# Ties between GpSimd and VectorE for a shared port: from the first quarter of an instruction list to all of it

## The chip, the core and the metric

The kernel runs on one core of a Trainium2 chip. The engines of the core are called here as the profile calls them: PE (TensorE, matmuls), DVE (VectorE), ACT (ScalarE), POOL (GpSimd) and SP (SyncE, which issues nearly all DMAs). Each engine works through its own instructions in order; between engines they wait on semaphores. The metric is the device time of one execution in microseconds (us); smaller is better. Three runs of the kernel before took 605.10, 605.38 and 605.64 us; the median is 605.38 us.

## The reference

What is computed is sparse attention (a band of local positions and a few global ones) over 4 batches, 8 heads, 768 positions of 64 numbers, followed by a layer norm and a two-layer feed-forward net that is added to its input. All in float32:

```python
scores = scale * np.matmul(q, k.transpose(0, 1, 3, 2))
scores = scores + bias[None, :, :, :]          # -slope of the head * distance
scores = np.where(keep, scores, -1000000000.0) # keep = is_global | is_local
a = np.exp(scores - np.max(scores, axis=-1, keepdims=True))
a = a / (np.sum(a, axis=-1, keepdims=True) + 1e-09)
x = np.matmul(a, v)                            # heads side by side: 4 x 768 x 512
xn = (x - mu) / np.sqrt(var + 1e-06) * g_ln
out = x + np.maximum(xn @ w_ch1, 0.0) @ w_ch2  # 512 -> 2048 -> 512
```

## The kernel before

The 4 x 768 positions are cut into 24 tiles of 128. For each tile `attention` (lines 604 to 690) loads q, k and v, splits each number into two float16 parts, gets scores on PE (line 641), takes the masked minimum on DVE (line 500) and the exponentials on ACT (line 505), splits these too (lines 646 and 647), has a DMA transpose them (line 649) and multiplies them with v (lines 468 to 470). Lines 664 to 698 are the layer norm and the transposes for the feed-forward net. The net is done for pairs of tiles. For the first pairs it is plain (`ffn1_alone`, `ffn1` and `ffn2`, lines 754 to 802 and 1042 to 1066); from the fifth pair on, `seven`, `twice` and `both_` (lines 805 to 1039) do two tiles with seven products in place of eight. These need sums and differences of weight blocks: `combine` (lines 704 to 748; line 716 adds, line 730 takes the low part) and `combine2` (lines 896 to 940; line 911 adds, line 932 takes the low part) build them, beside attention and plain net, on DVE and POOL. Tiles in SBUF live in one big tile, `arena`; PSUM tiles are `bank`.

**What sets the order.** Every step is recorded first (`Plan.op`) with the engine it is for, the time it is thought to take and, in `port`, whether it uses the port that DVE and POOL share. A table written out in the kernel (`STEPS`) gives the order of all 2,319 steps; a second one (`HOMES`) says which of DVE, ACT and POOL does a step that more than one could do. `Plan.times` (lines 158 to 175) works out a planned start for each, in which steps with `port` come one after another, never two at once. The instructions are then emitted in the order of the planned starts, so each engine's own order is fixed. A step of DVE that reads PSUM has `port` false, and so have small steps, such as line 476 or the `pow` of line 492 on POOL.

On the chip the engines do not keep to the planned times; only the order within an engine and the semaphores hold. `tied` (lines 1178 to 1189) adds one kind of semaphore wait that no data asks for. `ahead` holds the DVE step with `port` that was emitted last; the next POOL step with `port` waits until that one is done:

```python
if not o.port or at_ >= TIED:
    return o.emit()
...
if o.engine == "DVE":
    ahead[:] = [new[-1].name]
elif ahead:
    tc.add_manual_dep(new[0], ahead.pop(), SYNC, reason="port")
```

`at_` is the planned start in us. With `TIED = 150.0` this holds for about the first quarter of the list. A wait goes one way: POOL for DVE. A DVE step with `port` never waits for a POOL step in this manner.

Of the kernel before, what the change touches and what calls it, by code (L numbers as in the profile page):

```python
# [180 lines left out]
def banded(ctx, tc, q, k, v, n_global, n_local, g_ln, w1, w2, out, flag):  # L181
# [996 lines left out]
    def tied(at_, o):  # L1178

        if not o.port or at_ >= TIED:  # L1180
            return o.emit()
# [30 lines left out]
        emit(line[last:])  # L1212
    return found

TIED = 150.0
IDLE, HOLD, FILL = 3, 130.0, 0.9
CW = 4
ORDER = ["t01", "t23", "w0", "w1", "w2", "w3", "w4", "w5", "w6", "w7", "w8", "w9", "w10", "w11", "w12", "w13", "w14", "w15", *(f"a{t}{j}" for t in range(4) for j in range(4))]
# [318 lines left out]
```

## Time and profile before

| | |
|---|---|
| median of three runs | 605.38 us |
| the profiled execution, its own time | 604.78 us |
| its span (first to last instruction) | 603.0 us |
| PE busy | 588.1 us, 98% of the span |
| DVE busy | 517.4 us, 86% |
| ACT busy | 334.2 us, 55% |
| POOL busy | 230.3 us, 38%, 228 instructions |
| granted clock of PE | 0.997 of full speed over the span |

The profile is of one execution. Times in it are us from the start of the span. A row of the timeline gives start and duration, engine, line, operation, what is written and read with shapes, and in square brackets how long the engine was idle before and what ended that. A row of the waits says which instruction sat idle for which other one: total, times, longest. A row of the stretches gives the length and then the busy time of PE, of PE's weight loads, of DVE, ACT and POOL, each with its number of instructions, the granted clock of PE, the share of the DMA engines and GB/s.

### The profile page before, as it was taken

To read this page: it belongs to the slowest core of one execution; us is meant where nothing else is said; L and a number is where in the kernel's file an instruction comes from. 1 tells how busy PE (TensorE), PEld (TensorE's weight loads), DVE (VectorE), ACT (ScalarE), POOL (GpSimd) and SP (SyncE) were. 2 spreads that over 40 slices of the span, in tenths; PEclk is the share of its full clock that TensorE was granted. 3 is DMA by queue.
4 is the path that set the end of the run, shared out by engine and by line. 5 is a ranking of instruction groups with operands and counts; after the bars stand their busy time and mean duration, and the time that the engine had idled before them with its cause. 6 is when DMAs were issued, how large, how long until landed. Compare 5 with 4: busy or idle time off the path is not lost.

```text
span 603.0 us, 18624 instructions
## 1 busy us (share of the span) xinstructions
PE 588.1 (98%) x7657; PEld 513.3 (85%) x7657; DVE 517.4 (86%) x1147; ACT 334.2 (55%) x819; POOL 230.3 (38%) x228
## 2 busy tenths in 40 slices
PE   9899999999999999899999999999999999999995
PEld 7889987556778756788999999999999999998995
DVE  4999899989979999999997998988998897879661
ACT  4998887765635453663662872762664663551210
POOL 1315434145454353651541641352753441353100
PEclk9999999999999999999999999999999999999998
DMA  8995999987952967779889979987999796642201
GB/s 251 260 303 140 243 233 243 194 185 132 164 111 59 161 119 151 133 148 168 159 167 178 157 155 148 150 151 152 174 149 162 135 169 127 108 83 37 68 2 58
DMA packets 260268, 91.74 MB, mean 152 GB/s; under 512 B 250192, under 2 KB 250448, under 8 KB 260176
## 3 DMA queue, kind: packets, MB, share of 16 engines
q1 hardware_dynamic: 259888, 90.47, 77.2%
q8 instruction: 62, 1.02, 0.7%
q14 instruction: 30, 0.25, 0.2%
q10 hardware_dynamic: 288, 0.00, 0.0%
HBM read 38.01 MB, written 6.29 MB: 73 GB/s over the span
## 4 chain that ended last, share of the span: by engine, by line
PE 76%; DVE 14%; ACT 3%; issue 3%; DMA 2%; POOL 1%; SPq 0%; DVEq 0%; POOLq 0%; ACTq 0%
PE bank L973 13%; PE bank L954 11%; PE bank L1053 9%; PE bank L817 7%; PE bank L819 7%; PE bank L818 7%; PE bank L641 5%; PE bank L1174 2%; PE bank L794 2%; PE bank L792 2%; PE bank L793 2%; PE bank L766 2%; PE bank L764 1%; PE bank L765 1%; PE bank L468 1%
## 5 line engine op out<-in xcount | busy, mean ns | idle before, releaser
L203 ACT ACTIVATE arena<-arena 128x512 f16<-128x512 f32 (+3 forms) x115 | 69.3, 619 | 54.7 <-DVE arena L716 12.9
L203 ACT ACTIVATE arena<-bank 128x512 f16<-128x512 f32 (+1 forms) x95 | 55.3, 591 | 70.3 <-PE bank L819 41.8
L973 PE MATMUL bank<-w2h,arena 128*128 128x256 f16 x512 | 93.3, 273 | 0.0
L817 PE MATMUL bank<-arena 128*128 128x128 f16 x512 | 87.9, 219 | 1.2 <-ACT bank L203 1.1
L819 PE MATMUL bank<-arena 128*128 128x128 f16 x512 | 87.9, 219 | 0.0
L818 PE MATMUL bank<-arena 128*128 128x128 f16 x512 | 87.9, 219 | 0.0
L1053 PE MATMUL bank<-w2h,arena 128*128 128x512 f16 x256 | 81.7, 379 | 0.9 <-DVE x L1063 0.9
L505 ACT ACTIVATE arena<-arena,mn 128x256 f32<-128x256 f32 x160 | 80.0, 501 | 3.7
L973 PEld LDWEIGHTS <-arena 128*128 128x128 f16 x768 | 72.9, 98 | 7.8
L954 PEld LDWEIGHTS <-arena 128*128 128x128 f16 x672 | 63.8, 98 | 8.1 <-issue 0.7
L973 PE MATMUL bank<-w2l,arena 128*128 128x256 f16 x256 | 69.8, 273 | 0.0
L1053 PEld LDWEIGHTS <-arena 128*128 128x128 f16 x384 | 36.1, 98 | 38.6 <-issue 1.2
L817 PE MATMUL bank<-arena,w 128*128 128x128 f16 x384 | 66.7, 219 | 0.7 <-DVE arena L867 0.6
L819 PE MATMUL bank<-arena,w 128*128 128x128 f16 x384 | 66.8, 219 | 0.0
L818 PE MATMUL bank<-arena,w 128*128 128x128 f16 x384 | 66.7, 219 | 0.0
L647 POOL TENSOR_TENSOR arena<-arena 128x512 f16<-128x512 f32 x39 | 48.1, 1236 | 43.0 <-ACT arena L203 23.4
L500 DVE CUSTOM_DVE_ANT_0 arena<-bank,mask 128x256 f32<-128x256 f32 x160 | 59.8, 415 | 4.6 <-POOL arena L697 1.4
L818 PEld LDWEIGHTS <-arena 128*128 128x128 f16 x512 | 50.1, 98 | 1.7 <-issue 1.4
L817 PEld LDWEIGHTS <-arena 128*128 128x128 f16 x512 | 50.1, 98 | 0.3
L819 PEld LDWEIGHTS <-arena 128*128 128x128 f16 x512 | 50.0, 98 | 0.0
L641 PE MATMUL bank<-kT,qT 128*128 128x128 f16 x640 | 47.2, 219 | 1.7 <-DVE nm L500 1.4
L1053 PE MATMUL bank<-w2l,arena 128*128 128x512 f16 x128 | 48.5, 379 | 0.0
(215 smaller groups left out, 1798.1 us busy)
## 6 DMA issues: line engine op xcount, KB each, us to landing
arena<-in_moe_w_ch_dram SPq DMA_DIRECT2D x16, 1024.0 KB, 7.1
kf<-in_k_dram SPq DMA_DIRECT2D x28, 256.0 KB, 4.7
vf<-in_v_dram SPq DMA_DIRECT2D x28, 256.0 KB, 4.3
qf<-in_q_dram SPq DMA_DIRECT2D x24, 256.0 KB, 4.0
out_dram<-x SPq DMA_DIRECT2D x23, 256.0 KB, 2.9
qT<-qT SPq DMA_DIRECT2D x40, 128.0 KB, 3.5
pT<-arena SPq DMA_TRANSPOSE x80, 3.3
arena<-arena SPq DMA_TRANSPOSE x36, 3.2
```

The costliest lines, as they stand in the source:

```text
L203: act.activation(out=out(), in_=src(), func=AF.Relu if relu else AF.Copy, scale=by)
L500: vec.tensor_tensor_reduce(out=T()[:, u, :], in0=ps()[:, u], in1=mask(h), scale=1.0 / Z, scalar=3e38, op0=ALU.add, op1=ALU.min, accum_out= ...
L505: act.activation(out=T()[:, u, :], in_=T()[:, u, :], func=AF.Exp, scale=-1.0, bias=mn()[:, h:h + 1], accum_out=sm()[:, h:h + 1])
L641: pe.matmul(ps()[:, u, n_ * P:(n_ + 1) * P], lhsT=qT()[:, a * H + h, :], rhs=use[n_][0]()[:, h, :], start=(a == 0), stop=(a == 1))
L647: pick(pair(lambda eng, pn=pn, T=T: eng.tensor_tensor(out=pn()[:, :, 1, :], in0=T(), in1=pn()[:, :, 0, :], op=ALU.subtract), 512, "PD"), r ...
L766: pe.matmul(ps()[:, a], lhsT=wl, rhs=xT()[:, 0, kk, :], start=False, stop=(kk == NK - 1))
L817: pe.matmul(ps()[:, i, :], lhsT=wh, rhs=xT()[:, hi + kk, :], start=(first_ and i == 0 and kk == 0), stop=False, skip_group_check=True)
L818: pe.matmul(ps()[:, i, :], lhsT=wh, rhs=xT()[:, lo + kk, :], start=False, stop=False, skip_group_check=True)
L819: pe.matmul(ps()[:, i, :], lhsT=wl, rhs=xT()[:, hi + kk, :], start=False, stop=(i == 3 and kk == 1), skip_group_check=True)
L954: pe.matmul(ps(), lhsT=hh()[:, part, f, :], rhs=rhs, start=first_ and f == 0 and k == 0, stop=(f == 3 and k == 2), skip_group_check=True)
L973: pe.matmul(ps(), lhsT=hh()[:, part, i, :], rhs=w[:, f + i, n * K2:(n + 1) * K2], start=False, stop=(i == 3 and k == 2), skip_group_check= ...
L1053: pe.matmul(ps[t](), lhsT=h[:, part, :], rhs=w[:, f + a, :], start=(f + a == 0 and n_ == 0), stop=(f + a == NF - 1 and n_ == 2))
```

## The change

One constant is changed, so that `tied` holds for the whole list and not for what is planned ahead of 150 us:

```diff
-TIED = 150.0
+TIED = 1000.0
```

No instruction is added, removed or moved: the rows of each engine are the same and in the same order. What changes is what they wait for. After the first quarter 54 POOL instructions wait for a later DVE instruction than before; some that follow lose a DVE wait of their own, because it is now implied. Three places of POOL's list follow. `DVE_49`, `Activation_49`, `PE_49` and `Pool_49` are the semaphores on which these engines count their finished instructions, `DMAHW...` those of DMAs; a minus is the list before, a plus the list with the change.

POOL, where the sums of the second weights begin (it runs there at 200 to 215 us of the profile); line 911 adds weight blocks, 647 is the low part of the exponentials:

```order
 L716 TENSOR_TENSOR arena<-arena,w_01_92 128x512 [waits DVE_49]
 L911 TENSOR_TENSOR arena<-w2l,arena 128x512 [waits DVE_49,Activation_49]
-L911 TENSOR_TENSOR arena<-arena,w2h 128x512
+L911 TENSOR_TENSOR arena<-arena,w2h 128x512 [waits DVE_49]
 L932 TENSOR_TENSOR arena<-arena 128x512 [waits Activation_49]
-L647 TENSOR_TENSOR arena<-arena 128x2x256 [waits DMAHW6_49,DMAHW4_49,Activation_49]
+L647 TENSOR_TENSOR arena<-arena 128x2x256 [waits DMAHW4_49,DMAHW6_49,DVE_49,Activation_49]
 L932 TENSOR_TENSOR arena<-arena 128x512 [waits PE_49,Activation_49]
-L911 TENSOR_TENSOR arena<-w2l,arena 128x512 [waits DVE_49]
+L911 TENSOR_TENSOR arena<-w2l,arena 128x512
```

The second L911, free to start before, now waits for the DVE step written ahead of it, which is DVE's L911 on the other sum; the first L647 waits for a later L911 of DVE.

POOL, a little later (246 to 262 us), where the first pair of the seven-product net is prepared; lines 869 and 888 make operands for the second layer:

```order
 L647 TENSOR_TENSOR arena<-arena 128x2x256 [waits DMAHW5_49,Activation_49]
 L197 CAST arena<-arena 128x512 [waits PE_49,Activation_49]
-L869 TENSOR_TENSOR arena<-arena 128x512 [waits PE_49,Pool_49]
-L888 TENSOR_TENSOR arena<-arena 128x512 [waits DVE_49]
-L197 CAST arena<-arena 128x512 [waits PE_49,Pool_49]
+L869 TENSOR_TENSOR arena<-arena 128x512 [waits DVE_49,PE_49,Pool_49]
+L888 TENSOR_TENSOR arena<-arena 128x512
+L197 CAST arena<-arena 128x512 [waits DVE_49,PE_49,Pool_49]
 L197 CAST arena<-arena 128x512 [waits DVE_49]
 L869 TENSOR_TENSOR arena<-arena 128x512 [waits Pool_49]
```

The first L869 waits for DVE's own L869 (another operand), and the cast after it for the next one; L888, which reads what DVE wrote earlier, needs no wait of its own any more.

POOL at 386 to 396 us, in a later pair of the same net:

```order
 L647 TENSOR_TENSOR arena<-arena 128x2x256 [waits DMAHW6_49,DMAHW2_49,DVE_49]
-L869 TENSOR_TENSOR arena<-arena 128x512 [waits DVE_49,Activation_49]
+L869 TENSOR_TENSOR arena<-arena 128x512 [waits DVE_49]
 L197 CAST arena<-arena 128x2x256 [waits DMAHW1_49,Activation_49,Pool_49]
 L647 TENSOR_TENSOR arena<-arena 128x2x256 [waits Pool_49]
 L197 CAST arena<-arena 128x512 [waits DVE_49,Activation_49]
-L869 TENSOR_TENSOR arena<-arena 128x512 [waits Pool_49]
+L869 TENSOR_TENSOR arena<-arena 128x512 [waits DVE_49,Pool_49]
```

The first L869 waited for a DVE instruction before too, and now for a later one, DVE's second L869 of the pair, which implies what it needs of ACT; the second one gains a wait for a DVE copy.

## Rows read from the trace of the kernel before

**Rows 1.** The page: busy us, share of the span and instructions of each engine

```profile
PE 588.1 (98%) x7657; PEld 513.3 (85%) x7657; DVE 517.4 (86%) x1147; ACT 334.2 (55%) x819; POOL 230.3 (38%) x228
```

**Rows 2.** Stretches: length, busy PE, weight loads, DVE, ACT, POOL, clock, DMA, GB/s

```profile
200.00:275.00 75.00, 70.82 (x845) 53.16 (x843) 71.62 (x153) 38.69 (x106) 38.63 (x33) 1.00 0.76 138
275.00:550.00 275.00, 275.00 (x4145) 262.17 (x4144) 240.36 (x587) 147.40 (x404) 107.92 (x113) 1.00 0.85 147
550.00:603.00 53.00, 45.99 (x571) 42.17 (x569) 29.08 (x66) 7.57 (x14) 7.26 (x8) 0.97 0.15 40
```

**Rows 3.** Waits of PE: who waited for whom, us in total, times, longest

```profile
PE bank L641 <- DVE nm L500: 1.4, 1, 1.4
PE bank L817 <- ACT bank L203: 1.1, 1, 1.1
PE bank L1053 <- DVE x L1063: 0.9, 2, 0.8
PE bank L954 <- ACT bank L996: 0.6, 1, 0.6
PE bank L817 <- DVE arena L867: 0.6, 1, 0.6
PE bank L954 <- DVE arena L869: 0.3, 1, 0.3
```

**Rows 4.** The page's groups: busy us, mean ns of one matmul of line 1053

```profile
L1053 PE MATMUL bank<-w2h,arena 128*128 128x512 f16 x256 | 81.7, 379 | 0.9 <-DVE x L1063 0.9
```

**Rows 5.** The chain that ended last: six matmuls of line 1053 in a row

```profile
163.47 1.29 PE bank L1053 x6
```

**Rows 6.** DVE's groups at 200 to 275 us: busy us, mean ns, idle before

```profile
L911 DVE TENSOR_TENSOR arena<-arena,w2h 128x512 f32<-128x512 f32 x8 | 7.4, 919 | 0.1
L476 DVE TENSOR_SCALAR r<-sm 128x8 f32<-128x8 f32 x3 | 3.1, 1044 | 0.0
L869 DVE TENSOR_TENSOR arena<-arena 128x512 f16<-128x512 f32 x3 | 3.1, 1035 | 0.0
L730 DVE TENSOR_TENSOR arena<-arena 128x512 f16<-128x512 f32 x1 | 1.7, 1651 | 0.0
L911 DVE TENSOR_TENSOR arena<-w2l 128x512 f32<-128x512 f16 x2 | 1.4, 683 | 0.0
```

**Rows 7.** DVE's timeline at 200 to 275 us: start, duration, what

```profile
203.39 1.64 DVE L911 TENSOR_TENSOR arena<-arena,w2h 128x512 f32<-128x512 f32 x1
...
214.29 0.68 DVE L1063 SCALAR_TENSOR_TENSOR x<-bank,x 128x512 f32<-128x512 f32 x1
...
243.11 0.41 DVE L500 CUSTOM_DVE_ANT_0 arena<-bank,mask 128x256 f32<-128x256 f32 x1
...
246.90 1.09 DVE L647 TENSOR_TENSOR arena<-arena 128x512 f16<-128x512 f32 x1
...
255.03 1.75 DVE L869 TENSOR_TENSOR arena<-arena 128x512 f16<-128x512 f32 x1
...
272.34 1.10 DVE L614 SCALAR_TENSOR_TENSOR qn<-qf,qn 128x512 f16<-128x512 f32 x1
```

**Rows 8.** POOL's timeline at 200 to 275 us

```profile
202.88 1.61 POOL L911 TENSOR_TENSOR arena<-arena,w2h 128x512 f32<-128x512 f32 x1
...
242.60 1.60 POOL L911 TENSOR_TENSOR arena<-arena,w2h 128x512 f32<-128x512 f32 x1
...
253.40 1.16 POOL L869 TENSOR_TENSOR arena<-arena 128x512 f16<-128x512 f32 x1
...
271.71 1.18 POOL L197 CAST arena<-arena 128x512 f16<-128x512 f32 x1 [2.53 <-DMA arena<-arena]
```

**Rows 9.** DVE's and POOL's timelines at 390 to 393 us

```profile
390.26 1.47 POOL L869 TENSOR_TENSOR arena<-arena 128x512 f16<-128x512 f32 x1 [2.41 <-DVE arena L197]
390.03 2.24 DVE L869 TENSOR_TENSOR arena<-arena 128x512 f16<-128x512 f32 x2
...
392.80 0.67 DVE L872 SCALAR_TENSOR_TENSOR arena<-bank,arena 128x512 f32<-128x512 f32 x1
```

## The prediction

> **What bounds the kernel now.** I read the busy shares first. PE is busy for 98% of the span, DVE for 86% [rows 1], so only PE's idle time can be won, and the question is where that lies. The stretches answer it: from 275 to 550 us PE is busy for all of 275.00 us; from 200 to 275 us it is busy for 70.82 of 75, so 4.18 us are idle; from 550 to the end 45.99 of 53 [rows 2]. The first POOL step with a new wait runs at 155 us, so nothing ahead of that counts.
>
> The waits of PE say whom it waits for in those places. Six rows hold 4.9 us: 1.4 for a minimum of DVE (L500), 1.1 for a bank that ACT fills, 0.9 in two waits for DVE's L1063, 0.6 for another bank of ACT, and 0.6 and 0.3 for L867 and L869 of DVE [rows 3]. The first four rows lie between 215 and 275 us, the last two between 556 and 572 us. The other 6 us without PE after 550 are the program's end, which has no POOL in it. A wait costs more than its gap shows: a matmul of 512 columns is drawn with 379 ns [rows 4], but six of them follow each other in 1.29 us, 0.215 each [rows 5]. So the last matmul ahead of a gap is drawn 0.16 us too long, and seven gaps hide 1.1 us. The most that can be won is 4.9 + 1.1 = 6.0 us.
>
> In the stretch with most of these waits DVE is busy for 71.62 of 75 us, PE for 70.82, ACT and POOL for half [rows 2]. DVE is what PE waits for there, directly, or through steps of ACT that come behind DVE's.
>
> **What DVE loses to POOL.** One form of the sum on line 911 has a mean of 683 ns on DVE; the other form, of the same size, has 919 over eight instructions [rows 6]. One of the eight shows why: it starts at 203.39 and lasts 1.64 us, while POOL's own L911 runs from 202.88 to 204.49 [rows 7, 8]. Counted from POOL's end it needs 0.54 us. So DVE stood still for about 0.96 us, behind a POOL step that the list has after it. With 683 ns as the clean time of a 128x512 step the groups lose: L911 8 x 0.236 = 1.9 us, L869 3 x 0.352 = 1.1, L730 0.97. L476, only eight columns wide, lasts 1.04 us on the mean [rows 6]; if it needs no more than a step of 512 columns it loses at least 3 x 0.36 = 1.1. These four alone make 5.1 us of 75. A step that reads PSUM loses nothing: L500 at 243.11 has its 0.41 us [rows 7] in the middle of POOL's L911 of 242.60 to 244.20 [rows 8].
>
> **The change, part by part.** No instruction comes or goes. What is added is waiting on POOL.
>
> What the ties give. For each stall of DVE from 200 to 275 us I asked whether the POOL step that runs at the time has, with the change, a wait for that DVE step or a later one. For 13 it has, the first at 203.39, the last at 272.34 [rows 7]; counted against the shortest step of each form they hold 9.6 us. L476 at 229.1 and 250.3 has no tie (`port` is false there) and keeps its stall. DVE can thus gain up to 9.6 us in a stretch where PE needs 4.18 + 5 x 0.16 = 5.0 from it.
>
> What the ties take. 13 POOL steps of this stretch, the first at 202.88 and the last at 271.71 [rows 8], started before the DVE step that they will wait for had ended. Three as examples: L911 at 202.88 must wait for DVE's L911, which ended at 205.03, 2.15 us later; L911 at 242.60 for DVE's L647, which ended at 247.99, 5.4 later, the largest of all; L869 at 253.40 for DVE's L869, which ended at 256.78, 3.4 later [rows 7, 8]. Two things cut these delays. The DVE step itself ends sooner by its own stall (0.96, 0.41 and 1.07 us here), and DVE comes to it sooner by what it has gained until then. Behind the waiting step stands all of POOL's queue, and for that wait DMA transposes (behind L647), ACT (behind L869) and DVE (the sums). POOL has room: it is busy for 38.63 of 75 us, and for 107.92 of 275 later [rows 2]. I take the cost here as nothing, and the most as 3.4 us, the middle one of the three.
>
> What DVE does next. If its next step used the port too, that would stall behind the POOL step just let go, and the stall had only moved. In 12 of the 13 places the next DVE step reads a bank (L500, L1063, L480, L867, L872, L833, L776, L982); in about three a step with the port comes before POOL would be done. At some 0.7 us each that hands back 2 of the 9.6 us, which leaves more than the 5.0 that PE can use.
>
> The Trainium skill (SBUF — State Buffer, section "SBUF: two separate sides") has a rule that speaks against the change: whichever of DVE and GpSimd takes the shared pair of ports first has it for the whole instruction, and the other blocks in full. By that rule alone every collision keeps a loser, a tie only chooses which, and the sum would be near nothing. The trace agrees on the lock, with DVE's L911 done 0.54 us after POOL's; what it does not bear out is that the loser's time weighs the same on both, with DVE busy 95% and POOL 52% of the stretch.
>
> From 275 to 550 us there are 25 more POOL steps that the ties hold back, and PE has no gap to give back [rows 2]. There the ties can only cost, and cost nothing as long as the delay stays within POOL's slack. The tightest place that I found is at 390: POOL's L869 starts at 390.26 and ends at 391.73; the DVE step that reads its result, L872, starts at 392.80, 1.07 us later. With the change it waits for DVE's second L869, which ended at 392.27, a delay of 2.0 us [rows 9]. But 0.97 us of that was a stall behind this very POOL step, so 1.04 remain, about the slack.
>
> The sum, against the execution of 604.78 us. Upper end: all seven gaps close, 6.0 us. Lower end: no gap closes and delays overrun at several places (the last rival). I take all but the wait of 1.1 us for ACT's bank at 260.9: its chain runs through POOL's L869 and L888 at 253 to 256 us, which the ties hold back themselves. That leaves 6.0 - 1.1 - 0.16 = 4.8 us, so 600.0 us for such an execution. The median of the three runs lies 0.6 us above the profiled one: 605.4 - 4.8 = 600.6 us.
>
> **Rivals.**
> 1. Part of the gain. DVE cannot run ahead of PE, and what it wins early is lost again where it waits for PE's scores or ACT's exponentials. Then the first three small gaps close (0.9 and the 1.4, with 3 x 0.16), and the later ones stay: 2.8 us, 602.6 us. For it speaks that DVE's L500 reads scores which PE, never idle from 203 to 214 us, has just made; against it, that at 214.29 its L1063 is what PE waits for [rows 3, 7], so there DVE is behind and not ahead.
> 2. No change, 605.4 us. The stalls only move to DVE's next steps, or PE, having won 5 us by 275, loses them by 550 because DVE (240 of 275 us) cannot keep the lead. For it: DVE is at 87% there and several PE steps start right when DVE has let go. Against it: those are PE's own returns, which come sooner with PE.
> 3. Slower. The delays of POOL overrun their slack where PE has none: at 390 us POOL's L869 comes 2.0 us later, its slack is 1.07, so DVE's L872 and all of PE behind it come 0.9 us later [rows 9]. There are 25 held steps in that stretch of full PE; with such an overrun at three or four of them and nothing won, 3 us: 608.4 us. It decides where the DVE step waited for ends no sooner than now. Against it: nearly every such step is one whose end comes sooner without POOL in its way.
>
> **How the numbers follow.** My forecast, 599.4 to 602.0 us around 600.6, has 0.60; the part gain (602.0 to 604.2) 0.18; no change 0.10; slower 0.12. A difference of 0.2%, 1.2 us, is about what can be told from none. So faster 0.78, same 0.10, slower 0.12. The range reaches from 599.2 (the full 6.0 us, rounded down) to 604.2, which takes in the second case and leaves the last two out.
>
> **What would show it.** Right: PE busy for about 74 us in the 75 from 200 on and still without a gap after; the rows of L500, L1063 and L867 gone from PE's waits; DVE's means for L911 and L869 near 0.7 us; POOL waiting on DVE in new rows. L476 still near 1 us at times. Wrong: if the DVE groups get their clean times and PE's gaps stay, the gaps hung on something other than DVE; if new PE gaps appear between 275 and 550 behind L869, L647 or a transpose, the slack was too small; if the DVE means stay, the stalls have moved.

## The result, and the profile after

The changed kernel takes 598.48 us (median of 5 runs, 598.31 to 599.14). The kernel before, beside it on the same chip, takes 605.38 (5 runs, 604.58 to 605.79). The ratio is 0.9889, with a 95% interval of 0.9875 to 0.9904. The medians lie 6.9 us apart; by the ratio the gain is 6.7 us, between 5.8 and 7.6. The direction is the one forecast, but the time lies 2.1 us under the forecast of 600.6 and 0.7 under the low end, 599.2. The profiled execution took 598.57 us, span 596.8, granted clock 0.997.

The page's busy times, which answer to [rows 1]:

```profile
PE 586.7 (98%) x7657; PEld 513.6 (86%) x7657; DVE 501.9 (84%) x1147; ACT 334.1 (56%) x819; POOL 218.2 (37%) x228
```

The same instructions take 15.5 us less on DVE and 12.1 us less on POOL: both lost time to each other before. PE has its work as it had it. The stretches, with the columns of [rows 2] (the last one ends earlier, with the program):

```profile
200.00:275.00 75.00, 75.00 (x917) 57.80 (x915) 68.11 (x170) 41.79 (x117) 34.19 (x34) 1.00 0.82 149
275.00:550.00 275.00, 275.00 (x4136) 262.31 (x4134) 236.53 (x583) 145.56 (x395) 103.33 (x114) 1.00 0.81 144
550.00:597.00 47.00, 40.51 (x512) 37.53 (x510) 22.83 (x55) 6.48 (x12) 5.69 (x7) 0.96 0.16 45
```

PE is now busy for all of the 75 us where it had 70.82, and does 917 matmuls there instead of 845. From 275 to 550 us it stays full. Of the 47 us at the end it lacks 6.5, the end of the program. All that PE waits for in the whole execution:

```profile
PE bank L1174 <- DVE x L579: 1.5, 2, 1.0
PE bank L1174 <- DVE still L1205: 1.0, 1, 1.0
PE bank L440 <- DVE arena L199: 0.5, 1, 0.5
PE bank L766 <- POOL w L403: 0.4, 1, 0.4
PE bank L641 <- DMA qT<-qT: 0.3, 1, 0.3
```

None of the six rows of [rows 3] is left, and these five lie in the first 75 us. Line 1053 keeps its drawn 379 ns of [rows 4], with no idle time ahead of it.

The chain that ended last, by engine (PE had 76% and DVE 14% before): it now runs through PE nearly all the way.

```profile
PE 92%; DVE 4%; DMA 2%; ACT 1%; issue 0%; SPq 0%; DVEq 0%
```

DVE's groups at 200 to 275 us, to be held against [rows 6]:

```profile
L911 DVE TENSOR_TENSOR arena<-arena,w2h 128x512 f32<-128x512 f32 x8 | 5.4, 680 | 0.1
...
L869 DVE TENSOR_TENSOR arena<-arena 128x512 f16<-128x512 f32 x3 | 2.5, 820 | 0.1
...
L476 DVE TENSOR_SCALAR r<-sm 128x8 f32<-128x8 f32 x4 | 0.9, 235 | 0.0
L730 DVE TENSOR_TENSOR arena<-arena 128x512 f16<-128x512 f32 x1 | 0.7, 685 | 0.0
```

L911 goes from 919 to 680 ns, L730 from 1651 to 685, L476, of eight columns, from 1044 to 235. One L869 of the three still takes 1.08 us. The two L911 of [rows 7, 8] on DVE and on POOL, one fence for each engine:

```profile
203.64 0.68 DVE L911 TENSOR_TENSOR arena<-arena,w2h 128x512 f32<-128x512 f32 x1
```

```profile
204.40 1.15 POOL L911 TENSOR_TENSOR arena<-arena,w2h 128x512 f32<-128x512 f32 x1 [1.23 <-DVE arena L911]
```

POOL's step starts 1.5 us later than before, when DVE's is over, and takes 1.15 us where it took 1.61. DVE's takes 0.68 instead of 1.64.

Matched one by one with those of the trace before, PE's instructions are 0.2 us late up to 214 us, 1.0 us early by 225, 5.1 early by 275, steadily 5.1 to 5.2 until 550, and 6.3 at the end. So the time is won in the two places where PE had its gaps, and nothing of it is given back. 0.5 us of it is won at 250 and 252 us, in gaps too short for a row of the waits.

### The profile page after: what moved, and what is told of

Read it like the earlier page. It is cut to its first block, busy times and chain, and to the rows that moved or that the text cites. A ratio compares the mean times of both kernels' runs of the same rounds, so it can differ in the third digit from the quotient of the medians.

```text
span 596.8 us, 18645 instructions
## 1 busy us (share of the span) xinstructions
PE 586.7 (98%) x7657; PEld 513.6 (86%) x7657; DVE 501.9 (84%) x1147; ACT 334.1 (56%) x819; POOL 218.2 (37%) x228
## 4 chain that ended last, share of the span: by engine, by line
PE 92%; DVE 4%; DMA 2%; ACT 1%; issue 0%; SPq 0%; DVEq 0%
PE bank L973 14%; PE bank L1053 14%; PE bank L954 12%; PE bank L817 8%; PE bank L819 8%; PE bank L818 8%; PE bank L641 6%; PE bank L794 2%; PE bank L792 2%; PE bank L793 2%; PE bank L1174 2%; PE bank L468 2%; PE bank L470 2%; PE bank L469 2%; PE bank L766 2%; PE bank L764 2%
## 5 line engine op out<-in xcount | busy, mean ns | idle before, releaser
L647 POOL TENSOR_TENSOR arena<-arena 128x512 f16<-128x512 f32 x39 | 45.1, 1160 | 42.9 <-DVE r L476 10.6
```

What stands on the lines that cost most here:

```text
L647: pick(pair(lambda eng, pn=pn, T=T: eng.tensor_tensor(out=pn()[:, :, 1, :], in0=T(), in1=pn()[:, :, 0, :], op=ALU.subtract), 512, "PD"), r ...
```

## Experiments

Most change the same line of `tied`; `at_` is a step's planned start. In the trace of before POOL's sums and differences start between 2.6 us ahead of it and 6.6 us behind it. Letters A and B in the texts on record are the theory (the time is that of PE's gaps, and only the ties near a gap matter to it) and its rival in that text. Gains in us are the distance of the ratio from 1, times 605.

**Which ties carry the gain.** Those of the first quarter and of 200 to 270 alone:

```diff
-        if not o.port or at_ >= TIED:
+        if not o.port or not (at_ < 150.0 or 200.0 <= at_ < 270.0):
```

> Ties in the first quarter as before, and of the later ones only the 17 planned between 200 and 270 us (200 to 275 us of the trace). Theory A (PE's gaps come from DVE's stalls behind POOL in that stretch): the five gaps between 215 and 275 us close, 5.2 us are won, 600.2 us, and the two gaps of PE near 556 and 572 us stay, 1.1 us earlier or later than before by what is won. Theory B (POOL's work in planned order is worth something all along the list, stage by stage): 17 of the 72 later ties give 17/72 of 6.9 us, 1.6 us, 603.8 us.

Measured: 599.79 us (598.92 to 600.22), ratio 0.9912 [0.9899, 0.9925], a gain of 5.3 us. (In this kernel 16 of the 17 hold: the first has no DVE step with `port` of this stretch ahead of it.) The opposite, all ties but those of 200 to 270:

```diff
+        if not o.port or not (at_ < 200.0 or at_ >= 270.0):
```

> The complement: all ties but the 17 planned between 200 and 270 us. Theory A: the gaps of PE between 215 and 275 us stay as before, the two near 556 and 572 us close: 1.2 us won, 604.2 us. Theory B: 55 of the 72 later ties, 5.3 us won, 600.1 us.

Measured: 603.74 us (603.1 to 604.88), ratio 0.9984 [0.9975, 0.9993], a gain of 1.0 us. The waits of PE after 150 us, first in the one and then in the other, with the stretch from 200 to 275 of each:

```profile
PE bank L817 <- DVE arena L867: 0.6, 1, 0.6
...
PE bank L954 <- DVE arena L869: 0.3, 1, 0.3
200.00:275.00 75.00, 75.00 (x917) 57.79 (x915) 68.08 (x169) 41.78 (x117) 34.18 (x34) 1.00 0.82 149
```

```profile
PE bank L641 <- DVE nm L500: 1.4, 1, 1.4
...
PE bank L1053 <- DVE x L1063: 0.9, 2, 0.8
PE bank L817 <- ACT bank L203: 0.9, 2, 0.6
PE bank L954 <- ACT bank L996: 0.6, 1, 0.6
200.00:275.00 75.00, 71.39 (x851) 53.73 (x850) 71.58 (x154) 38.69 (x106) 38.05 (x33) 1.00 0.75 138
```

Each set closes the gaps near it and leaves the listed ones of the other, and the two gains add up to 6.3 of the 6.7 us of all ties. In both kernels PE also loses 0.4 us between 350 and 500 us, which it does not lose with all ties. Theory A holds in both.

**Is DVE's time what PE was short of?** All ties, and beside them extra work for DVE in the stretch, a maximum of a 128x512 tile that nobody reads, after 9 or after all 17 of the tied steps there (`EACH`):

```diff
+            if 200.0 <= at_ < 270.0:
+                seen.append(at_)
+                if len(seen) % 2 or EACH:
+                    vec.tensor_reduce(out=scratch, in_=gb, axis=AX.X, op=ALU.max)
```

> All ties, and behind every second of the 17 ties planned between 200 and 270 us one more DVE instruction: a maximum over 512 columns of the tile gb into a scratch column that nobody reads, about 0.6 us each, nine of them, 5 us of DVE. POOL waits as in the changed kernel. Theory A (DVE's time): DVE was given back 9.2 us of stall in the stretch and PE needed 5.2 of them, so about 4 us of lead are spare; 5 us of filling cost 0.5 to 2 us, 599 to 600.5 us, with a first small gap of PE between 215 and 275 us. Rival (POOL's later start itself is what helps, for ACT, DMAs or the order): 598.5 us, no gap.

> The same behind each of the 17 ties: about 10 us of DVE, a little more than the stalls that went. Theory A: the gaps of PE between 215 and 275 us come back, 4 to 6.5 us in all, 602.5 to 605 us, with POOL's waits as in the changed kernel. Rival (POOL's later start itself): 598.5 us, at most 1 us more.

With nine: 599.42 us (599.16 to 599.74), ratio 0.9904 [0.9889, 0.9919], 0.9 us less gain than without them, with intervals that overlap, and no wait of PE is listed in the stretch (it is busy for 74.78 of the 75 us). This one is in line with the theory but decides nothing alone. With 17: 601.66 us (600.82 to 602.06), ratio 0.9938 [0.9923, 0.9952], 3.0 us of the gain gone. One such step takes 0.68 us, so nine are 6.1 us and 17 are 11.6; DVE had 6.9 us free in the stretch. The 17's waits of PE and the stretch:

```profile
PE bank L641 <- DVE nm L500: 1.1, 2, 0.8
...
PE bank L817 <- DVE bank L833: 0.6, 1, 0.6
200.00:275.00 75.00, 72.91 (x875) 55.18 (x873) 72.96 (x177) 39.54 (x110) 34.17 (x34) 1.00 0.76 142
```

PE waits for DVE again, though not at the places of [rows 3]: matched with all ties, it loses its time in several gaps between 231 and 262 us, and none at 215. The cost is about 1 us under the low end of what was expected, but it goes the way of the theory, and the rival (at most 1 us) falls: PE is short of DVE's time, whatever that is lost to.

**The wait that the sum left out.** The prediction kept the gap at 260.9 us open, because its chain runs through two POOL steps that the ties hold back. Here the ties of 249 to 270 are left out, those from 200 to 249 kept (nine in this kernel, where the text counts 11):

```diff
+        if not o.port or not (at_ < 150.0 or 200.0 <= at_ < 249.0):
```

> Ties in the first quarter, and of the later ones only the 11 planned between 200 and 249 us; those at 250 to 270 us, among them the two that hold POOL's casts and L869 ahead of PE's gap at 260.9, are gone. The prediction left that gap open since those ties hold POOL's own L869 and L888. If it was right on this, the gap closes here at least as well as in the fully tied kernel. Theory A (DVE's lead decides, held POOL steps or not): the gaps at 215, 222 and 244 us close, 2.8 us; those at 260.9 and 274.8 close in part, as DVE stalls again by 3.8 us there but comes with a lead of some 2 us: 1 of 2 us. 601.6 us, between 600.8 and 602.6.

Measured: 601.32 us (601.01 to 601.97), ratio 0.9933 [0.992, 0.9946], 1.3 us less gain than with the ties up to 270 (0.9912, with an interval that just overlaps). The gaps at 260.9 and 274.8 are there:

```profile
PE bank L817 <- ACT bank L203: 0.7, 1, 0.7
PE bank L954 <- ACT bank L996: 0.6, 1, 0.6
```

The first is shorter than in [rows 3], but this proves nothing: in the second profile of the kernel before, below, it is 0.6. With the ties up to 270 both gaps are gone, so the ties in question close them. How they close the one at 260.9, the timelines show. First the kernel before, POOL, DVE and ACT:

```profile
254.52 1.71 POOL L888 TENSOR_TENSOR arena<-arena 128x512 f32<-128x512 f32 x1
```

```profile
259.46 0.69 DVE L872 SCALAR_TENSOR_TENSOR arena<-bank,arena 128x512 f32<-128x512 f32 x1
```

```profile
260.25 0.58 ACT L203 ACTIVATE bank<-bank 128x512 f32<-128x512 f32 x1 [0.52 <-DVE arena L872]
```

PE goes on at 260.88, when ACT's copy has filled its bank. The copy needs DVE's L872 to be done with that bank, and L872 reads what POOL's L888 wrote. L888 was done at 256.23, 3.2 us before L872 began: the gap hung on DVE, not on POOL. Without the ties in question:

```profile
250.17 1.16 POOL L869 TENSOR_TENSOR arena<-arena 128x512 f16<-128x512 f32 x1
251.29 1.72 POOL L888 TENSOR_TENSOR arena<-arena 128x512 f32<-128x512 f32 x1
```

```profile
250.60 1.28 DVE L647 TENSOR_TENSOR arena<-arena 128x512 f16<-128x512 f32 x1
251.80 1.76 DVE L869 TENSOR_TENSOR arena<-arena 128x512 f16<-128x512 f32 x1
...
256.24 0.69 DVE L872 SCALAR_TENSOR_TENSOR arena<-bank,arena 128x512 f32<-128x512 f32 x1
```

```profile
257.02 0.58 ACT L203 ACTIVATE bank<-bank 128x512 f32<-128x512 f32 x1 [0.52 <-PE bank L470]
```

and with them, in the kernel with the ties up to 270:

```profile
251.86 1.16 POOL L869 TENSOR_TENSOR arena<-arena 128x512 f16<-128x512 f32 x1 [1.97 <-DVE arena L869]
252.98 1.28 POOL L888 TENSOR_TENSOR arena<-arena 128x512 f32<-128x512 f32 x1
```

```profile
250.41 0.68 DVE L647 TENSOR_TENSOR arena<-arena 128x512 f16<-128x512 f32 x1
251.01 0.68 DVE L869 TENSOR_TENSOR arena<-arena 128x512 f16<-128x512 f32 x1
...
254.91 0.69 DVE L872 SCALAR_TENSOR_TENSOR arena<-bank,arena 128x512 f32<-128x512 f32 x1
```

```profile
255.69 0.58 ACT L203 ACTIVATE bank<-bank 128x512 f32<-128x512 f32 x1 [0.27 <-PE bank L819]
```

POOL's L869 starts 1.69 us later, and L888 ends 1.25 us later, at 254.26. But DVE's two steps end at 251.69 instead of 253.56, 1.87 us earlier, and L872 starts 1.33 us *earlier*, still after L888. ACT's copy, 1.33 us earlier too, starts 0.09 us after L872's end in both (its bracket names PE, whose signal came a few hundredths later still).

**Profiled run and median.** The kernel before once more, one profile, nothing changed, to see what differs between two of its executions.

> The kernel before, unchanged, profiled once more. The profiled execution of before took 604.78 us, the median of its runs 605.38. If the 0.6 us between them are time in which PE waits (theory A), then the time of this execution less that of the first profile equals the difference of PE's gaps between 200 and 603 us to about 0.2 us, wherever it falls. If they lie outside (start, end, or the first 150 us), PE's gaps after 200 us are 6.0 us again whatever the time is.

Measured: 604.02 us, span 602.2, 0.76 us less than the first profile. Matched one by one, PE's instructions are 0.1 us late up to 250 us and 0.7 us early from 262 us to the end. One row of [rows 3] shows most of it:

```profile
PE bank L817 <- ACT bank L203: 0.6, 1, 0.6
```

It was 1.1. The rest is won at 252 us, in a gap too short for a row. So these two executions differ by PE's waits, which the change takes away too.

**Without the first quarter.** Ties only from 150 us on (`at_ >= 150.0`), and none at all (`at_ < 0.0`):

> Ties only from 150 us of the plan on; the 24 of the first quarter are gone. Theory A: in the first quarter PE's gaps lie ahead of 75 us, where loads and the start set them, and PE has none between 75 and 200 us; DVE's stalls grow by 2 to 4 us there, but PE's end moves by 0 to 1 us against the fully tied kernel: 598.5 to 599.5 us. Theory B: each tie is worth the same, 6.9/72 us, so 2.3 us are lost: 600.8 us.

> No tie at all. Theory A: as the kernel before, later by what the first quarter's ties are worth to PE, 0 to 1 us: 605.4 to 606.4 us, with PE's gaps between 215 and 275 us as before. Theory B: 2.3 us slower than before, 607.7 us.

Both missed. Ties from 150: 609.3 us (606.35 to 610.46), ratio 1.0066 [1.0046, 1.0087]. None: 614.8 us (612.09 to 615.8), ratio 1.0154 [1.0134, 1.0173]. The 24 ties of the first quarter are worth 10.7 us when the later ones are there, more than the 72 that the change adds, though some 3 us of this go with PE's clock (last section). The PE waits that come or grow in the first (the first row was 1.5), none of them after 150 us:

```profile
PE bank L1174 <- DVE x L579: 3.5, 2, 2.5
PE bank L764 <- DVE arena L776: 2.0, 2, 1.5
PE bank L567 <- DVE x L579: 2.0, 1, 2.0
```

Why so much, DVE's and POOL's timelines of this kernel show:

```profile
21.41 1.59 DVE L392 SCALAR_TENSOR_TENSOR arena<-arena 128x1024 int32<-128x1024 int32 x1
22.92 3.23 DVE L384 TENSOR_SCALAR arena<-arena 128x1024 uint16<-128x1024 uint16 x1
```

```profile
22.00 3.00 POOL L403 TENSOR_TENSOR w<-arena,w 128x1024 f16<-128x1024 f32 x1
```

With all ties L384 takes 1.31 us there and POOL's L403 2.14. Here POOL starts at 22.00, can get on only when DVE's L392 ends at 23.00, and DVE's next step stands until POOL is done at 25.00: it ends 1.15 us after that. Two more kernels price these ties, with `at_ >= 35.0` (three left out, L403 twice) and `at_ >= 75.0` (ten left out, L403 six times):

> All ties but the three of the plan's first 35 us, which hold a 128x1024 cast and two 128x1024 subtractions of POOL (lines 197 and 403). Theory A (the price of a tie left out is the stretch that VectorE then loses behind one POOL step, where PE has nothing else to do): in the kernel whose ties begin at 150 the two 128x1024 VectorE steps at 22.9 and 29.3 us took 3.23 and 3.14 us instead of 1.31 and 1.22, so 1.9 us each; PE loses 3.8 us less what its slack there takes: 600.5 to 602.5 us. Rival (the ten microseconds of the first quarter come from PE's granted clock, which was 0.95 on the mean there, or from the weight loads that start late): three ties make no more than their share of 24, near 1.3 us: 599.5 to 600.

> All ties but the ten of the plan's first 75 us, six of which hold 128x1024 subtractions of POOL's line 403. Theory A (each such tie saves one VectorE step some 1.9 us, and PE waits for VectorE there): the time comes near the kernel whose ties begin at 150, 606 to 608 us, and the fourteen ties between 75 and 150 are worth only the 1 to 3 us that are left. Rival (every tie of the first quarter is worth about the same, 10.8 us over 24): 603 us.

Measured: 601.76 us (600.95 to 602.52), ratio 0.9955 [0.9938, 0.9971], and 606.93 us (606.38 to 607.8), ratio 1.0037 [1.0024, 1.0049]. By these ratios three ties are worth 4.0 us, ten 9.0, the other fourteen of the quarter 1.8 (with intervals that overlap). DVE's two groups of 20 such steps in the first 75 us, with the three left out and then with all ties:

```profile
L392 DVE SCALAR_TENSOR_TENSOR arena<-arena 128x1024 int32<-128x1024 int32 x10 | 15.4, 1552 | 0.9 <-ACT arena L388 0.9
L384 DVE TENSOR_SCALAR arena<-arena 128x1024 uint16<-128x1024 uint16 x10 | 15.2, 1521 | 0.0
```

```profile
L392 DVE SCALAR_TENSOR_TENSOR arena<-arena 128x1024 int32<-128x1024 int32 x10 | 13.4, 1350 | 0.9 <-ACT arena L388 0.9
L384 DVE TENSOR_SCALAR arena<-arena 128x1024 uint16<-128x1024 uint16 x10 | 13.2, 1323 | 0.0
```

DVE takes 4.0 us more, nearly all of it in two steps of 3.23 and 3.15 us. PE does not lose all of that: this profile is of the fastest of the four executions, 600.95 us, and in it PE's instructions fall 2.0 us behind those of the kernel with all ties after the first of the two steps, 1.1 more after the second, and end 2.6 us late. That DVE's 4.0 us equal the 4.0 us of the ratio is a coincidence; part of the latter goes with PE's clock (last section). What a tie saves here is the stretch that DVE stands behind one POOL step, less PE's slack. Per tie the rest of the quarter is worth far less, so the rival of equal shares falls. No kernel tried beats the one with all ties, and after 75 us its profile lists no wait of PE any more.

## Why the prediction was right in its way and short in its size

**What bounds it: right.** Only PE's idle time could be won, and where it lay. The gain sits in the five gaps of 200 to 275 us (5.3 us with the ties of that stretch alone) and the two at the end (1.0 with the others alone).

**What DVE loses to POOL: right but for L476.** The groups come near their clean times. Counted against the shortest step of each form, DVE's stalls of 200 to 275 us fall from 14.1 to 5.0 us; 9.1 are won where 9.6 less 2 handed back were forecast. Extra work of the size of DVE's free time costs little while more brings PE's waits back. On L476 the prediction was off. At least 1.1 us for three was low: the shortest L476 takes 0.16 us, so the three lost about 2.6 us, and a narrow step lost as much behind POOL (0.96) as a wide one. And the two without a tie, at 229.1 and 250.3, did not keep their stall: they take 0.17 and 0.45 us now, as POOL's steps have moved away from them. One L476 of 0.93 us stands elsewhere, at 467.9.

**Against the rule of the lock: right.** The trace without early ties shows the whole-instruction lock in both directions, as the Trainium skill (SBUF — State Buffer, "SBUF: two separate sides") has it: POOL's 2.14 us became 3.00 behind DVE and DVE's 1.31 became 3.23 behind POOL. That a tie then only chooses the loser, and the sum is nothing, is not what the runs show: both engines lose less, DVE 15.5 and POOL 12.1 us of busy time over the whole program. POOL waits on a semaphore instead, and has the slack; DVE gains.

**The cost of the ties on POOL, taken as nothing: right.** From 275 to 550 us no PE gap came. At the place of [rows 9] POOL's L869 now starts at 386.29, after DVE's, and DVE does wait for its result:

```profile
384.92 1.29 DVE L869 TENSOR_TENSOR arena<-arena 128x512 f16<-128x512 f32 x2
...
387.49 0.69 DVE L872 SCALAR_TENSOR_TENSOR arena<-bank,arena 128x512 f32<-128x512 f32 x1 [0.47 <-POOL arena L869]
```

L872 is nonetheless 5.31 us earlier than before, as PE is. DVE's 2.24 for the two L869 are 1.29, and that pays for the delay. The third rival named the place rightly; its price did not come.

**The sum: the step that failed.** The prediction: "I take all but the wait of 1.1 us for ACT's bank at 260.9: its chain runs through POOL's L869 and L888 at 253 to 256 us, which the ties hold back themselves." The dependence is there, but it was taken for the link on which the gap hung. DVE's L872, which reads what L888 wrote, began 3.2 us after L888 had ended; it was late because DVE's own L647 and L869 had stood behind POOL. A held POOL step had to be compared with that slack, and not with its old start: L888 ends 1.25 us later with the ties, L872 starts 1.33 us earlier. The kernel without just those ties keeps this gap; with them it is closed. That is 1.26 of the 2.1 us.

This alone would have given 599.4 us, inside the range. That the time fell under the range's low end, 599.2, lies in the ceiling: "The most that can be won is 4.9 + 1.1 = 6.0 us." The medians show 6.9 (5.8 to 7.6 by the ratio's interval, so the last 0.7 us is not clear of noise). Part of it the traces show. The profiled executions differ by 604.78 - 598.57 = 6.2 us, 0.2 over the ceiling: from 200 us on PE gained 6.6 us, the 6.0 of the seven gaps and 0.5 in gaps too short for a row of the waits, and the stretch ahead gave 0.2 back. The other 0.7 us is the step from profile to median. The 0.6 us by which the median lay over the profiled run was carried over to the result as if it were a constant; after the change the two agree (598.48 and 598.57). The second profile of before shows its executions differing by PE's waits, so the 0.6 us may have been such waits, or the scatter of three runs: beside the experiments the kernel before had medians of 604.97 (17 runs), 605.12 (11) and 604.74 (9), all within 0.4 us of the profiled 604.78. The runs behind the median left no trace, so which it was stays open. The low end took the same frame, 605.4 less 6.0, and so left the time out. If every wait can close, the low end is PE's own work, and then the largest gain counts from the median.

## What to carry to other kernels

When DVE and POOL share a port and DVE is what the bound engine waits for, let POOL wait by a semaphore for the DVE step that the order puts ahead of it: POOL's loss goes into its slack, and DVE's goes away. Judge a held step by when its consumer can start, with DVE's regained time counted in, not by its own later start. For the best case, take the bound engine's work as the floor and set it against the median of the runs, as waits too short to be listed (0.5 us here), and perhaps those that vary from run to run, go with the rest.

## What the runs showed of the hardware beside this

One POOL step of 2.14 us in the wrong place costs a DVE step 1.9 us, and two of them made PE 2.6 us late in the profiled execution.

In the kernel whose ties begin at 150 us, PE's waits in the head go with a lower granted clock; the stretch from 25 to 75 us of it:

```profile
25.00:50.00 25.00, 22.50 (x192) 18.86 (x192) 23.26 (x32) 19.18 (x33) 7.76 (x7) 0.93 0.86 251
50.00:75.00 25.00, 22.37 (x311) 21.46 (x309) 22.84 (x39) 17.00 (x30) 11.46 (x7) 0.93 0.60 149
```

With all ties PE is busy for 24.44 and 24.29 us of these stretches, at 1.00. 0.93 on the mean means that some of each stretch ran at the lower of the two levels (1.2 and 2.4 GHz). Ahead of the first fall PE had stood still for 2.5 us and ahead of the second for 2.0 us, both times for L579. The kernel with three ties left out has the first of these waits too, and 1.00 in both stretches of its profiled execution. What the clock costs can be estimated: 0.07 of 25 us is 1.75 us a stretch if PE was busy in it, so up to 3.5 of the 10.5 us by which this execution (609.03 us) is longer than that with all ties. The runs agree: of the six executions the one at 0.998 over its span took 606.35 us, the five at 0.990 to 0.993 took 608.12 to 610.46; without any tie it is 612.09 at 0.999 and 614.21 to 615.80 at 0.992 to 0.993. So about 3 us go with the clock and the rest with the waits themselves. The 4.0 us of the three ties have a part of it too: the executions at 0.999 took 600.95 and 601.60 us, those at 0.995 and 0.994 took 601.93 and 602.52.
